# Attention with a 32-bit P: eight tiles with later low-half products, and two of sixteen steps with P as one float

## The chip, the cores and the metric

The kernel runs on one core of one Trainium2 chip. The metric is device time in microseconds. The core's engines are called as in the profile: PE (TensorE, matrix products), PEld (its weight loads), DVE (VectorE), ACT (ScalarE), POOL (GpSimd) and SP (SyncE, which starts transfers).

## The reference

The computation is one transformer-like layer with 2048 rows of 512 features, modulated by a condition vector `c`. Attention has 32 heads of 16 features, all in float32:

```
mod = (silu(c) @ w_mod) split into sa, ca, ga, sb, cb, gb
h   = layernorm(x) * (1 + ca) + sa
q, k, v = split(h @ A_wqkv)                 # 32 heads of 16
p   = softmax(q k^T * 0.25)                 # 2048 x 2048 per head
x   = x + ga * ((p v) @ A_wo)
h   = layernorm(x) * (1 + cb) + sb
x   = x + gb * mixer(h)                     # gelu layers w1, w2 with shifts, then w3, w4
```

## The kernel before

The kernel keeps nearly float32 accuracy while it uses fast matmul forms. Weights and activations are split into a high and a low part in fp32r, and three products replace one fp32 product.

Attention is cut into 64 **units** (`units`, line 946): four chunks of 512 queries times 16 pairs of heads. A unit has 16 **steps**, one per 128 keys, and a step has two **half-steps**, one per head of the pair (j = 0, 1). A half-step does two things on PE, as a *row pair*: the scores of its own step (`score_part`, tile `sc`, line 1012) and, 24 steps ahead (`LEAD`), scores in the other orientation for a coming unit's row maxima (`max_part`, tile `mb`, line 996). The two use different halves of the array's rows. DVE reduces `mb` to maxima (line 992). ACT takes the exponential of `sc` and writes it as a 32-bit integer into a tile of P, `pt` (line 1008); the exponent is shifted so that the integer has up to 26 bits.

P times V then goes in two halves of that integer. The high 16 bits are read in place as fp16 numbers; four matmuls per step (line 1086, one **group**, 32 columns each and hence side by side in the array) multiply them with V, which is held in three bf16 parts (`vst`). The low 16 bits are first made fp16 in place by `p_low` on POOL (line 1061), or on ACT (lines 1058 and 1059, shown in the profile as L156) when POOL's planned clock is more than 200 ns behind ACT's. One group of four matmuls per *pair* of steps multiplies them (line 1083). All products of a unit add up in one PSUM bank, `pv`. After the unit ACT copies it to `ac` (line 1103), PE sorts it (`ot`, line 1113), and ACT, DVE and POOL divide by the row sums (lines 1120 to 1128). The next unit's first group waits for that copy.

There are eight PSUM banks: one for `pv`, seven shared by `sc`, `mb` and `ot`. Tiles of P come from a ring of six (`NPT`).

The order of instructions on every engine is written out by a planner in Python (`Sched`), which keeps a clock per engine from fixed costs (a row pair 232 ns, a group 240, a maximum 605, an exponential 480, a low half 1345 on POOL and 1150 on ACT; a transfer its bytes at 360 per ns, then 2200 ns). Engines run their instructions in that order. The main loop (line 1602) goes by **blocks** of three half-steps (`GRP`): three row pairs, then the groups that are due. What is due stands in the list `pvs` (line 1600): for each pair of steps the high group of the first, that of the second, then the low group. An entry is taken two blocks (`LAG`) after its half-step has passed: half-step 2s for the first high group, 2s + 2 for the second and for the low group. V for a unit is fetched six steps ahead (`load_v`), Q and K 32 steps ahead.

The query chunks' remaining work (output projection, mixer) is the *tail*. Its memory pool `fa` is set up at the end of unit 15, but it is used only near the end of attention and after it, with tiles `xn`, `xf` and `xb` among others.

Of the kernel before, what the change touches and what calls it, by code (L numbers as in the profile page):

```python
# [105 lines left out]
LNG = (1, 3)  # L106
LNC = 2
VP = 2
XB = 4


# [219 lines left out]
def kernel(ctx, tc, A_x, A_wqkv, A_wo, B_w1, B_w2, B_w3, B_w4, c, w_mod, out):  # L331
# [635 lines left out]
            load_rows(kst[u % 3], j, Ks, h, slice(0, S), slice(0, S))  # L967

    def load_v(u):
        vst[u] = at.tile([P, NKT, 192], BF16, name="vst", tag="vst", bufs=2)  # L970
        sch.dma(dma.dma_start, vst[u], Vs[units[u][1]])

    sm = Slots(NSM)
    e_exp, e_hi, e_low, v_free, acs = {}, {}, {}, [0.0], []

    def bank(nm):
# [3 lines left out]
    def max_part(m, j):  # L980
# [14 lines left out]
                max_fin(u)  # L995
        return ready, lambda: te.matmul(b, lhs, kst[u % 3][r, c * CH:(c + 1) * CH], start=True, stop=True), after  # L996

    def score_part(s, j):

        u, kt = divmod(s, NKT)  # L1000
        if j == 0:
            pt[s] = at.tile([P, 2, CH], I32, name="pt", tag="pt", bufs=NPT)
        x, b = bank("sc")
        ready, sm.t[x] = sm.t[x], LATE
        r = slice(64 * j, 64 * j + 64)

        def after(e):
            ea = sch.crit("A", 480, e + PX, lambda: act.activation(pt[s][:, j], b, AF.Exp))  # L1008
            sm.t[x] = ea + XP["A"]
            if j:  # L1010
                e_exp[s] = e_hi[s] = ea
        return ready, lambda: te.matmul(b, kst[u % 3][r, kt * P:(kt + 1) * P], qst[u][r], start=True, stop=True), after  # L1012

    def row_pair(s, j):
# [48 lines left out]

    def pv_ready(s, lo):

        return max(e_low[s], e_low[s + 1]) if lo else max(e_hi.pop(s), v_free[0] if s % NKT == 0 else 0.0)

    def pv_part(s, lo):


        u, kt = divmod(s, NKT)
        if kt == 0 and not lo:
            pv[u] = ap_.tile([P, CH], F32, name="pv", tag="v", bufs=1)
        v, acc = vst[u], pv[u]

        def mms():
            for j in range(2):
                for i in range(2):
                    r = 64 * j + 32 * i
                    if lo:  # L1080
                        c = 128 + 32 * j + (0 if i else 8)
                        n = min(32, 192 - c)
                        te.matmul(acc[r:r + n, :], v[:, kt + i, c:c + n].bitcast(F16), pt[s + i].bitcast(F16)[:, j, 0::2],  # L1083
                                  start=False, stop=kt == NKT - 2, skip_group_check=True)
                    else:
                        te.matmul(acc[r:r + 32, :], v[:, kt, r:r + 32], pt[s].bitcast(F16)[:, j, 1::2],  # L1086
                                  start=kt == 0, stop=False, skip_group_check=True)
# [135 lines left out]
    def pool_of(ci):  # L1223
        return fa if ci < NB or (ci - NB) % 2 else tp
# [58 lines left out]
    def tail(ci):  # L1283
# [91 lines left out]
        def normed(key, t, rs):  # L1375
            tag = xtag(key, t)
            xlive[tag] = xlive.get(tag, 0) + 1
            x = xn[key, t] = (tp if tag == "x4" else fa).tile([P, D], F32, name="xn", tag=tag, bufs=XN[tag])
            y = xbt[t]
            return ln_apply(x, y, rs), mark((key, t))  # L1380

# [15 lines left out]
        for i, t in enumerate(new):  # L1397
            yield lambda: ci != 1 or i < HOLD or ("xn4", 2) in done
            yield lambda: sch.room() and xn_room("xn", t) and t in x1t and sch.now() >= arr.get(("x1", t), 0.0) and (ci < 2 or ("z", t - 2 * TPC) in done)
            yield from wo_mm(i, range(KT))  # L1400
            b = banks.pop(i)
            x1 = x1t[t]
            xb = xbt[t] = pool_of(ci).tile([P, D], F32, name="xb", tag="xb", bufs=XBF if pool_of(ci) is fa else XBT)

            def x1_add(x1=x1, b=b):
                dve.tensor_tensor(x1, x1, b, op=OP.add)
                sch.free(b)

            r, m, ops = ln_ops(x1, True)
            r2, ops2 = ln_ops(xb)  # L1410

            def center(xb=xb, x1=x1, m=m, ops=ops):
                ops[0][2]()
                sch.late = sch.put("G", 464, sch.T["D"] - cD() + XX, ops[1][2]) + XX
                dve.scalar_tensor_tensor(xb, x1, m[:, 0:1], cbrow, op0=OP.subtract, op1=OP.mult)
# [181 lines left out]


    blocks = [list(range(i, min(i + GRP, 2 * NS))) for i in range(-2 * LEAD, 2 * NS, GRP)]
    pvs = [x for s in range(0, NS, 2) for x in ((s, 0), (s + 1, 0), (s, 1))]  # L1600
    due = 0.0
    for k, blk in enumerate(blocks + [[]] * (LAG + CPER)):
        if blk and blk[0] <= LENDS <= blk[-1]:
            sch.most = MOST
        for x in blk:
            if x % 2 == 0:
                if x == blk[0]:
                    before(x // 2)
                if x >= 0 and x % 32 == 0:
                    drain(("shift", x // 32))  # L1610
        if acs:
            ac_copy()
        row = [divmod(x, 2) for x in blk if x < 2 * NS]
        s0 = row[0][0] if row else 0
        col = []
        if k >= LAG and (k % CPER == 0 or not blk):

            x = (blocks[min(k - LAG, len(blocks) - 1)] or [-1])[-1]
            while pvs and 2 * (pvs[0][0] + pvs[0][1]) < x and not (col and pvs[0][0] % NKT == 0 and not pvs[0][1]):
                col.append(pvs.pop(0))  # L1620
        t, start = CIN, 0.0
        need = sum((s >= 0) + (s + LEAD < NS) for s, _ in row)
        sch.flush(need)
        banks = sorted(sm.t)
        n = 0
        for s, i in row:
            n += (s >= 0) + (s + LEAD < NS)

            start = max(start, banks[n - 1 + 2 * (s < 0)] - t)
            t += CROW  # L1630
        t += CMID
        for s, i in col:
            start = max(start, pv_ready(s, i) - t)
            t += CCOL
        sch.gap(start)
        sch.flush(need)
        sch.T["P"] = max(sch.T["P"], start) + CIN
        low = sorted(e_exp)
        for s, i in row:
            for fn in row_pair(s, i):  # L1640
                fn()
        for x in blk[1:]:
            if x % 2 == 0:
                before(x // 2)
        for s in low:
            p_low(s)
        sch.T["P"] += CMID
        for s, i in col:
            pv_part(s, i)
        sch.T["P"] += COUT  # L1650
        for e in "ADG":
            sch.misc(e, max(sch.T["P"], sch.T[e]) + TOLE[e])
        if s0 < 0:
            sch.fill(LEADB / 2 * len(blk))
        elif sch.gens:
            late = s0 >= NS - T0S
            due += RATE3 if late else RATE if s0 < NS // NC else RATE2
            if due >= (BURST3 if late else BURST if s0 < NS // NC else BURST2):
                sch.fill(due)
                due = 0.0  # L1660
        if 2 * (NS // NC) - 1 in blk:
            for key in (("v", 1), ("kq", 3), ("q", 0), ("q", 1), "pieces"):
                drain(key)
            qpx.close()
            sch.gapmin = GAPMIN2
            ot = o0x.enter_context(tc.tile_pool(name="ot", bufs=1, side="right"))
            for ci in range(1, NC):
                oh[ci] = ot
                osb[ci] = ot.tile([P, TPC, D], F32, name=f"osb{ci}", tag=f"osb{ci}", bufs=1)
            fa = o0x.enter_context(tc.tile_pool(name="fa", bufs=1, side="right"))  # L1670
            big = {"A4": fa.tile([P, 4 * KT * 2 * P], F32R, name="A")}
            big["A"] = big["A4"]
        if blk and blk[0] <= 2 * (NS - T0L) <= blk[-1]:
            sch.add(tail_loads())
        if blk and blk[0] <= 2 * (NS - T0S) <= blk[-1]:
            sch.add(tail(0))
# [54 lines left out]
```

## Time and profile before

| | |
|---|---|
| median of 3 runs | 2019.44 us (2016.7 to 2020.83) |
| profiled execution | span 2019.7 us; the profile gives no other time of it |
| instructions | 41655 |
| PE busy | 1934.4 us, 96% |
| DVE busy | 1656.3 us, 82% |
| ACT busy | 1510.2 us, 75% |
| POOL busy | 1571.9 us, 78% |
| PE's granted clock | 0.992 of full speed |

The shares are over the whole span. The first part (to about 500 us) mixes projections with attention, the middle is attention alone, and after about 1500 us comes the tail, in which PE works almost alone. A change to attention is to be read in the middle. In the lists of groups a row gives line, engine, operation, tiles (written <- read), shapes and count, then busy time in us and the mean duration in ns, then the idle time before it and who ended it. A matmul's duration includes its way through the array; how far apart matmuls start says what they cost.

### The profile page before, as it was taken

To read this page: it belongs to the slowest core of one execution; us is meant where nothing else is said; L and a number is where in the kernel's file an instruction comes from. 1 tells how busy PE (TensorE), PEld (TensorE's weight loads), DVE (VectorE), ACT (ScalarE), POOL (GpSimd) and SP (SyncE) were. 2 spreads that over 40 slices of the span, in tenths; PEclk is the share of its full clock that TensorE was granted. 3 is DMA by queue.
4 is the path that set the end of the run, shared out by engine and by line. 5 is a ranking of instruction groups with operands and counts; after the bars stand their busy time and mean duration, and the time that the engine had idled before them with its cause. 6 is when DMAs were issued, how large, how long until landed. Compare 5 with 4: busy or idle time off the path is not lost.

```text
span 2019.7 us, 41655 instructions
## 1 busy us (share of the span) xinstructions
PE 1934.4 (96%) x14456; PEld 1162.1 (58%) x14456; DVE 1656.3 (82%) x2979; ACT 1510.2 (75%) x3085; POOL 1571.9 (78%) x1488
## 2 busy tenths in 40 slices
PE   7999999999999999999999999999998999999999
PEld 5755545454444444444444444444455878898998
DVE  6398888879999999999999999999975886556443
ACT  6438987768999999999999999999985544344443
POOL 6349988879999999999999999999996554435222
PEclk9989999999999999999999999999999999999999
DMA  8777675445343434444443435354414676553541
GB/s 295 233 204 192 151 187 155 135 130 124 86 92 87 91 88 83 96 82 97 81 98 75 104 72 107 72 136 126 99 46 158 230 261 265 226 200 116 201 153 68
DMA packets 185508, 278.01 MB, mean 138 GB/s; under 512 B 117104, under 2 KB 127856, under 8 KB 169008
## 3 DMA queue, kind: packets, MB, share of 16 engines
q1 hardware_dynamic: 181792, 267.20, 49.1%
q10 hardware_dynamic: 2304, 4.20, 0.6%
q0 software_dynamic: 1200, 3.93, 0.5%
q8 instruction: 115, 1.88, 0.4%
q14 instruction: 97, 0.79, 0.1%
HBM read 211.81 MB, written 62.91 MB: 136 GB/s over the span
## 4 chain that ended last, share of the span: by engine, by line
PE 61%; DVE 16%; ACT 9%; issue 6%; POOL 4%; DMA 3%; SPq 0%; ACTq 0%; POOLq 0%; DVEq 0%
PE mb L996 13%; DVE mx L992 12%; PE pv L1086 9%; PE sc L1012 8%; ACT pt L1008 7%; PE w L363 5%; PE w L359 5%; PE w L361 5%; PE pv L1083 4%; PE ot L1113 3%; POOL pt L1061 2%; PE xT L1247 1%; POOL trs L1356 1%; PE v L359 1%; DMA wr<-Ws 1%
## 5 line engine op out<-in xcount | busy, mean ns | idle before, releaser
L1061 POOL TENSOR_SCALAR pt<-pt 128x1024 f16<-128x1024 uint16 x953 | 1248.3, 1367 | 79.9 <-ACT pt L1008 76.7
L992 DVE TENSOR_REDUCE mx<-mb 128x1 f32<-128x512 f32 x2048 | 1250.0, 681 | 72.7 <-PE mb L996 63.5
L1008 ACT ACTIVATE pt<-sc 128x512 int32<-128x512 f32 x2048 | 1060.9, 614 | 123.5 <-PE mb L996 97.1
L996 PE MATMUL mb<-kst,qtl 62*128 62x512 f32 x2048 | 781.1, 461 | 20.5 <-ACT pt L1008 10.0
L1012 PE MATMUL sc<-qtl,kst 64*128 64x512 f32 x2048 | 739.3, 449 | 4.6 <-DVE mx L992 1.8
L996 PEld LDWEIGHTS mb<-kst,qtl 62*128 62x128 f32 x2048 | 358.9, 193 | 233.7 <-ACT pt L1008 160.4
L1012 PEld LDWEIGHTS sc<-qtl,kst 64*128 64x128 f32 x2048 | 336.6, 185 | 185.4 <-DVE mx L992 118.7
L1086 PE MATMUL pv<-pt,vst 128*32 128x512 f16 x4096 | 384.8, 397 | 20.6 <-ACT ac L1103 20.6
L1460 POOL TENSOR_TENSOR g<-sq,g 128x256 fp32r<-128x256 f32 (+1 forms) x124 | 96.8, 785 | 188.9 <-ACT g L1459 176.6
L1083 PE MATMUL pv<-pt,vst 128*32 128x512 f16 (+1 forms) x2048 | 220.8, 389 | 2.5 <-POOL pt L1061 2.4
L1086 PEld LDWEIGHTS <-vst 128*32 128x32 bf16 x4096 | 91.8, 93 | 227.2 <-issue 208.8
L361 PE MATMUL w<-A,wr 128*128 128x256 f32 (+1 forms) x520 | 153.4, 295 | 0.3 <-DVE A L349 0.3
L359 PE MATMUL w<-A,wr 128*128 128x256 f32 (+1 forms) x520 | 153.2, 295 | 0.3 <-ACT A L353 0.3
L363 PE MATMUL w<-A,wr 128*128 128x256 f32 (+1 forms) x520 | 153.1, 294 | 0.0
L1456 ACT ACTIVATE sq<-w 128x256 f32<-128x256 f32 (+1 forms) x130 | 52.1, 401 | 127.0 <-PE w L363 117.5
L363 PE MATMUL w<-wr,g 128*128 128x512 f32 x270 | 106.5, 394 | 3.1 <-POOL g L1460 3.1
L359 PE MATMUL w<-wr,g 128*128 128x512 f32 x270 | 106.9, 396 | 1.8 <-DMA wr<-Ws 1.8
L361 PE MATMUL w<-wr,g 128*128 128x512 f32 x270 | 106.1, 393 | 0.0
L1438 DVE SCALAR_TENSOR_TENSOR sq<-sq,w 128x256 f32<-128x256 f32 (+1 forms) x130 | 58.1, 449 | 56.5 <-ACT sq L1458 56.3
L359 PEld LDWEIGHTS w<-A,wr 128*128 128x128 f32 x520 | 98.7, 190 | 1.7 <-ACT A L353 0.5
L361 PEld LDWEIGHTS w<-A,wr 128*128 128x128 f32 x520 | 98.7, 190 | 1.6 <-DVE A L349 0.5
L363 PEld LDWEIGHTS w<-A,wr 128*128 128x128 f32 x520 | 98.6, 190 | 0.5 <-issue 0.5
(156 smaller groups left out, 2131.6 us busy)
## 6 DMA issues: line engine op xcount, KB each, us to landing
wr<-Ws SPq DMA_DIRECT2D x66, 1024.0 KB, 5.2
vst<-Vs SPq DMA_DIRECT2D x64, 768.0 KB, 5.7
kst<-Ks SPq DMA_DIRECT2D x126, 384.0 KB, 6.1
Ws<-wr SPq DMA_DIRECT2D x14, 1024.0 KB, 5.0
qtl<-Qs SPq DMA_DIRECT2D x128, 96.0 KB, 4.3
Vs<-vt SPq DMA_DIRECT2D x32, 384.0 KB, 4.2
Ks<-qk SPq DMA_DIRECT2D x16, 512.0 KB, 3.8
Qs<-qk SPq DMA_DIRECT2D x16, 512.0 KB, 3.0
```

Source lines behind the costliest of these rows:

```text
L359: te.matmul(o, lh, rh, start=first, stop=False)
L361: te.matmul(o, lh, rl, start=False, stop=False)
L363: te.matmul(o, ll, rh, start=False, stop=last)
L992: end = sch.crit("D", 605, e + PX, lambda: dve.reduce_max(mxs[u][:, j, g, c:c + 1], b, axis=AX.X))
L996: return ready, lambda: te.matmul(b, lhs, kst[u % 3][r, c * CH:(c + 1) * CH], start=True, stop=True), after
L1008: ea = sch.crit("A", 480, e + PX, lambda: act.activation(pt[s][:, j], b, AF.Exp))
L1012: return ready, lambda: te.matmul(b, kst[u % 3][r, kt * P:(kt + 1) * P], qst[u][r], start=True, stop=True), after
L1061: e_low[s] = XP["G"] + sch.crit("G", 1345, ready, lambda: pool.tensor_scalar(o, i, 0.5, 1.0, op0=OP.mult, op1=OP.mult))
L1083: te.matmul(acc[r:r + n, :], v[:, kt + i, c:c + n].bitcast(F16), pt[s + i].bitcast(F16)[:, j, 0::2], start=False, stop=kt == NKT - 2, skip ...
L1086: te.matmul(acc[r:r + 32, :], v[:, kt, r:r + 32], pt[s].bitcast(F16)[:, j, 1::2], start=kt == 0, stop=False, skip_group_check=True)
L1113: te.matmul(b[:, t * n:(t + 1) * n], ac[:, t * P:(t + 1) * P], smat.rearrange("p j d -> p (j d)"), start=True, stop=True)
L1460: ("G", cG(n), lambda: pool.tensor_tensor(lo, sq, hi, op=OP.subtract)), (None, 0, end), bank=b)
```

## The change

First, the ring of P tiles has eight members from step 264 to 983: six as before and two laid into the tail's tiles `xn` and `xf`, which are empty then. In the same steps the low group of a pair of steps is due up to three half-steps later (not for the last pair of a unit).

Second, in units 17 to 60 the steps 4 and 5 of the 16 are handled otherwise (`full`). ACT writes the exponential of such a step as one float per element into `pfull` (in the tail's `xb`); there is no low half, and it takes no tile of the ring. V of these two key tiles is made once per unit on POOL: `vfull` is the three bf16 parts of V as float32, times 2^-40, queued by `load_v` when the transfer of V is planned to have landed. Instead of the high groups and the low group of the two steps (three groups of four matmuls) there are four parts (`pv_full`), two per step. Each part covers 256 of the 512 queries and consists of two fp32 products, 64 output rows per head. Their gates are half-steps 1, 4, 7 and 10 after the first of the two steps, so they fall into different blocks as a rule; the planner charges 460 ns each.

The tail's `xn`, `xf` and `xb` become fixed slices of three tiles, with as many slots as before, so that the loans above are possible. The diff without that last part:

```
+WIDE = range(S // CH * 64 + 8, 984)
+LOWLAG = 3
+FU = range(17, 61)
+FK = 4
+FGATE = (1, 4, 7, 10)
+CFULL = 460.0
...
     def load_v(u):
-        vst[u] = at.tile([P, NKT, 192], BF16, name="vst", tag="vst", bufs=2)
-        sch.dma(dma.dma_start, vst[u], Vs[units[u][1]])
+        v = vst[u] = at.tile([P, NKT, 192], BF16, name="vst", tag="vst", bufs=2)
+        e = sch.dma(dma.dma_start, v, Vs[units[u][1]])
+        if u in FU:
+            sch.chain(("G", 360, lambda: pool.tensor_scalar(vfull[u % 2], v[:, FK:FK + 2, 0:128], 2.0 ** -20, 2.0 ** -20,
+                                                            op0=OP.mult, op1=OP.mult)), prio=0, ready=e)
+
+    def full(s):
+        return s // NKT in FU and s % NKT in (FK, FK + 1)
...
+    def new_pt(s):
+        if s in WIDE:
+            i = pn[0] % (NPT + len(ptx)) - NPT
+            pn[0] += 1
+            if i >= 0:
+                pt[s] = ptx[i]
+                return
+        pt[s] = at.tile([P, 2, CH], I32, name="pt", tag="pt", bufs=NPT)
...
-        if j == 0:
-            pt[s] = at.tile([P, 2, CH], I32, name="pt", tag="pt", bufs=NPT)
+        if full(s):
+            p = pfull[s % 2][j]
+        else:
+            if j == 0:
+                new_pt(s)
+            p = pt[s][:, j]
...
-            ea = sch.crit("A", 480, e + PX, lambda: act.activation(pt[s][:, j], b, AF.Exp))
+            ea = sch.crit("A", 480, e + PX, lambda: act.activation(p, b, AF.Exp))
             sm.t[x] = ea + XP["A"]
             if j:
-                e_exp[s] = e_hi[s] = ea
+                e_hi[s] = ea
+                if not full(s):
+                    e_exp[s] = ea
...
+    def pv_full(s, n):
+
+        u, kt = divmod(s, NKT)
+        c = slice(256 * n, 256 * n + 256)
+
+        def mms():
+            for j in range(2):
+                r = slice(64 * j, 64 * j + 64)
+                te.matmul(pv[u][r, c], vfull[u % 2][:, kt - FK, r], pfull[s % 2][j][:, c], start=False, stop=False,
+                          skip_group_check=True)
+        sch.put("P", CFULL, 0.0, mms)
...
-    pvs = [x for s in range(0, NS, 2) for x in ((s, 0), (s + 1, 0), (s, 1))]
+    pvs = []
+    for s in range(0, NS, 2):
+        if full(s):
+            pvs += [(2 * s + x, s + i // 2, 2 + i % 2) for i, x in enumerate(FGATE)]
+            continue
+        low = 2 * s + 2 + (min(LOWLAG, 2 * (NKT - 2 - s % NKT)) if s in WIDE else 0)
+        pvs += [(2 * s, s, 0), (2 * s + 2, s + 1, 0), (low, s, 1)]
+    pvs.sort(key=lambda x: x[0])
...
+            pfull += [[xbs[:, 2 * i + j] for j in range(2)] for i in range(2)]
+            vfull += [xns["xn"][:, 2, 256 * i:256 * i + 256].rearrange("p (k d) -> p k d", k=2) for i in range(2)]
+            ptx += [x[:, 0:2].bitcast(I32) for x in xns.values()]
```

More of the change, by code (lines that the diff above doesn't have):

```diff
@@ L969, in load_v @@
     def load_v(u):
-        vst[u] = at.tile([P, NKT, 192], BF16, name="vst", tag="vst", bufs=2)
-        sch.dma(dma.dma_start, vst[u], Vs[units[u][1]])
+        v = vst[u] = at.tile([P, NKT, 192], BF16, name="vst", tag="vst", bufs=2)
[5 more added lines that the diff above has]
+        return s // NKT in FU and s % NKT in (FK, FK + 1)
     sm = Slots(NSM)
+    ptx = []
+    vfull, pfull = [], []
     e_exp, e_hi, e_low, v_free, acs = {}, {}, {}, [0.0], []
@@ L996, in max_part @@
         return ready, lambda: te.matmul(b, lhs, kst[u % 3][r, c * CH:(c + 1) * CH], start=True, stop=True), after
+    pn = [0]
+    def new_pt(s):
[6 more added lines that the diff above has]
+        pt[s] = at.tile([P, 2, CH], I32, name="pt", tag="pt", bufs=NPT)
     def score_part(s, j):
         u, kt = divmod(s, NKT)
-        if j == 0:
-            pt[s] = at.tile([P, 2, CH], I32, name="pt", tag="pt", bufs=NPT)
+        if full(s):
[4 more added lines that the diff above has]
+            p = pt[s][:, j]
         x, b = bank("sc")
@@ L1064, in pv_ready @@
     def pv_ready(s, lo):
+        if lo > 1:
+            return e_hi[s]
         return max(e_low[s], e_low[s + 1]) if lo else max(e_hi.pop(s), v_free[0] if s % NKT == 0 else 0.0)
+    def pv_full(s, n):
[7 more added lines that the diff above has]
+        sch.put("P", CFULL, 0.0, mms)
     def pv_part(s, lo):
@@ L1377, in normed @@
             xlive[tag] = xlive.get(tag, 0) + 1
-            x = xn[key, t] = (tp if tag == "x4" else fa).tile([P, D], F32, name="xn", tag=tag, bufs=XN[tag])
+            if tag == "x4":
+                x = tp.tile([P, D], F32, name="xn", tag=tag, bufs=XN[tag])
+            else:
+                x = xns[tag][:, xnum[tag] % XN[tag]]
+                xnum[tag] += 1
+            xn[key, t] = x
             y = xbt[t]
@@ L1402, in tail @@
             x1 = x1t[t]
-            xb = xbt[t] = pool_of(ci).tile([P, D], F32, name="xb", tag="xb", bufs=XBF if pool_of(ci) is fa else XBT)
+            xb = xbt[t] = xbs[:, t % XBF] if pool_of(ci) is fa else tp.tile([P, D], F32, name="xb", tag="xb", bufs=XBT)
             def x1_add(x1=x1, b=b):
@@ L1618 @@
             x = (blocks[min(k - LAG, len(blocks) - 1)] or [-1])[-1]
-            while pvs and 2 * (pvs[0][0] + pvs[0][1]) < x and not (col and pvs[0][0] % NKT == 0 and not pvs[0][1]):
-                col.append(pvs.pop(0))
+            while pvs and pvs[0][0] < x and not (col and pvs[0][1] % NKT == 0 and not pvs[0][2]):
+                col.append(pvs.pop(0)[1:])
         t, start = CIN, 0.0
@@ L1633 @@
             start = max(start, pv_ready(s, i) - t)
-            t += CCOL
+            t += CFULL if i > 1 else CCOL
         sch.gap(start)
@@ L1648 @@
         for s, i in col:
-            pv_part(s, i)
+            if i > 1:
+                pv_full(s, i - 2)
+            else:
+                pv_part(s, i)
         sch.T["P"] += COUT
@@ L1671 @@
             big = {"A4": fa.tile([P, 4 * KT * 2 * P], F32R, name="A")}
+            xbs = fa.tile([P, XBF, D], F32, name="xbs")
+            xns = {k: fa.tile([P, XN[k], D], F32, name=k) for k in ("xn", "xf")}
+            xnum = {"xn": 0, "xf": 0}
+            pfull += [[xbs[:, 2 * i + j] for j in range(2)] for i in range(2)]
+            vfull += [xns["xn"][:, 2, 256 * i:256 * i + 256].rearrange("p (k d) -> p k d", k=2) for i in range(2)]
+            ptx += [x[:, 0:2].bitcast(I32) for x in xns.values()]
             big["A"] = big["A4"]
```

## The prediction

> **What bounds the kernel now.** I read the busy time by stretches first. In the middle of attention nothing is idle; where it ends, everything but PE thins out.
>
> ```profile
> 600.00:700.00 100.00, 96.50 (x824) 45.54 (x824) 96.14 (x168) 92.87 (x185) 95.66 (x83) 1.00 0.43 91
> ...
> 1500.00:1600.00 100.00, 88.37 (x548) 66.69 (x545) 67.17 (x133) 55.20 (x113) 64.95 (x83) 0.97 0.45 159
> ```
>
> PE, PE's loads, DVE, ACT and POOL stand in that order. Four engines at 93 to 97% do not say which one sets the pace, so the second view is the groups of instructions from 600 to 1400 us, pure attention.
>
> ```profile
> L992 DVE TENSOR_REDUCE mx<-mb 128x1 f32<-128x512 f32 x1257 | 764.1, 681 | 26.7 <-PE mb L996 21.0 <-PE sc L1012 2.9
> L1128 DVE RECIPROCAL rc<-sm 128x8 f32<-128x8 f32 x39 | 7.6, 195 | 5.7 <-ACT sm L1120 5.7
> L1042 DVE TENSOR_REDUCE mf<-mx 128x8 f32<-128x32 f32 x39 | 7.0, 180 | 0.1
> ...
> L1061 POOL TENSOR_SCALAR pt<-pt 128x1024 f16<-128x1024 uint16 x577 | 751.1, 1363 | 27.2 <-ACT pt L1008 25.0
> L1124 POOL TENSOR_TENSOR osb<-sm,rc 128x128 f32<-128x128 f32 x39 | 15.9, 409 | 2.8 <-DVE rc L1128 2.8
> L1045 POOL TENSOR_TENSOR nm<-mf,nm 128x8 fp32r<-128x8 f32 x39 | 7.9, 203 | 2.3 <-ACT nm L1044 2.0
> ...
> L1008 ACT ACTIVATE pt<-sc 128x512 int32<-128x512 f32 x1257 | 648.4, 615 | 47.4 <-PE mb L996 39.0 <-PE sc L1012 2.0 <-POOL pt L1061 0.8
> L156 ACT ACTIVATE pt<-pt 128x1024 f16<-128x1024 uint16 x53 | 72.9, 1375 | 0.0
> L1103 ACT ACTIVATE ac<-pv 128x512 f32<-128x512 f32 x39 | 24.3, 624 | 0.0
> ```
>
> A unit (one head pair against one query chunk, 16 steps) has 32 maxima, so the window holds 1257 / 32 = 39.28 units of 800 / 39.28 = 20.37 us, and a block (three half-steps, 1.5 steps) takes 1.91 us. The chain of waits has a piece in which DVE alone sets the pace:
>
> ```profile
> 1224.05 17.87 DVE mx L992 x30
> ```
>
> That is 17.87 / 30 = 0.596 us per maximum, 1.79 us per block. DVE therefore needs 32 x 0.596 + 0.195 + 0.180 = 19.45 us per unit and loses 0.92. POOL works (751.1 + 15.9 + 7.9) / 39.28 = 19.73 us per unit: 577 / 39.28 = 14.7 low halves and two small operations; the other 53 / 39.28 = 1.35 low halves go to ACT. DVE is the floor, POOL and ACT sit right under it. The waits of that window show how the 0.92 us arise:
>
> ```profile
> PEld mb L996 <- ACT pt L1008: 115.8, 340, 0.8
> PEld sc L1012 <- DVE mx L992: 84.8, 219, 0.5
> ...
> PE pv L1086 <- ACT ac L1103: 15.2, 13, 1.2
> ```
>
> PE's loads wait for PSUM banks that ACT or DVE has not emptied, and every third unit PE stops for the copy of the accumulator. One such stop in order of time, ACT, then DVE, then PE:
>
> ```profile
> 849.51 1.35 ACT L156 ACTIVATE pt<-pt 128x1024 f16<-128x1024 uint16 x1
> 850.71 0.60 ACT L1103 ACTIVATE ac<-pv 128x512 f32<-128x512 f32 x1
> ```
>
> ```profile
> 845.33 6.66 DVE L992 TENSOR_REDUCE mx<-mb 128x1 f32<-128x512 f32 x11
> 852.71 1.89 DVE L992 TENSOR_REDUCE mx<-mb 128x1 f32<-128x512 f32 x3 [0.72 <-PE mb L996]
> ```
>
> ```profile
> 847.47 0.49 PE L1012 MATMUL sc<-qtl,kst 64*128 64x512 f32 x1
> ...
> 848.38 0.41 PE L1086 MATMUL pv<-pt,vst 128*32 128x512 f16 x4
> 848.62 0.40 PE L1083 MATMUL pv<-pt,vst 128*32 128x512 f16 x4
> 848.94 0.50 PE L996 MATMUL mb<-kst,qtl 62*128 62x512 f32 x1
> ...
> 849.69 0.51 PE L996 MATMUL mb<-kst,qtl 62*128 62x512 f32 x1
> ...
> 851.35 0.64 PE L1086 MATMUL pv<-pt,vst 128*32 128x512 f16 x8 [1.16 <-ACT ac L1103]
> ...
> 852.14 0.50 PE L1012 MATMUL sc<-qtl,kst 64*128 64x512 f32 x1
> ...
> 853.25 0.41 PE L1086 MATMUL pv<-pt,vst 128*32 128x512 f16 x4
> 853.60 1.08 PE L1113 MATMUL ot<-smat,ac 128*128 128x34 f32 x8
> 854.61 0.51 PE L996 MATMUL mb<-kst,qtl 62*128 62x512 f32 x1
> ...
> 855.50 0.41 PE L1086 MATMUL pv<-pt,vst 128*32 128x512 f16 x4
> 855.74 0.40 PE L1083 MATMUL pv<-pt,vst 128*32 128x512 f16 x4
> 855.97 0.41 PE L1086 MATMUL pv<-pt,vst 128*32 128x512 f16 x4
> 856.30 0.50 PE L1012 MATMUL sc<-qtl,kst 64*128 64x512 f32 x1
> ```
>
> A low half on ACT holds up the accumulator's copy; PE idles 1.16 us, and DVE runs dry for 0.72 us. The same rows give PE's own need: an unstalled block with two groups of P V products takes 848.94 - 847.47 = 1.47 us, with three 856.30 - 854.61 = 1.69 us. So a block is about 1.01 us plus 0.23 per group. DVE's 1.79 us leave PE 0.1 to 0.3 us per block. That margin decides this case.
>
> **The change, part by part.** The page gives no time of the profiled execution but its span, 2019.7 us; the median of the three runs is 2019.44, so I work from 2019.7. The runs spread over 0.2%, about what a measurement of this kernel can tell from no change. Units 17 to 60 are changed: 44 units.
>
> *Relief of POOL and ACT.* Two of 16 low halves per unit disappear: 2 x 1.30 = 2.6 us (751.1 / 577). One operation that scales V comes in, 128 x 256. No row shows it; the nearest are a smaller one, L1124 above (128 x 128, 0.41 us), and one of its size with two inputs:
>
> ```profile
> L787 POOL TENSOR_TENSOR vt<-vr,vt 128x256 bf16<-128x256 f32 x32 | 22.6, 710 | 36.6 <-ACT vt L786 36.4
> ```
>
> I take 0.55 us, between the two. With all 14 low halves on POOL its work is 14 x 1.30 + 0.40 + 0.20 + 0.55 = 19.35 us, just under DVE's floor. The planner charges POOL 16 x 1345 + 600 = 22.1 us per unit now and, at 20.4 us, must hand (22.1 - 20.4) / 1.345 = 1.3 low halves to ACT, which the trace confirms (1.35). With the change it charges 14 x 1345 + 600 + 360 = 19.8 us. Fourteen steps in a row still build up a backlog, so I expect not zero but some 0.7 on ACT. Worth: at most DVE's whole 0.92 us per unit, at least nothing (if another wait is late next). I take the stop at the accumulator, 15.2 / 39.28 = 0.39 us per unit. Once it goes, the bank waits on DVE's maxima are late next.
>
> *P as one float.* The exponentials keep shape and source; L1103 writes float from the same shape in 0.624 us against 0.615, so nothing. PE loses three groups per unit (four high and two low halves' products are one group per high step and one per low pair): 3 x 0.23 = 0.69 us. It gains four parts, each of two fp32 products of 256 columns. What one costs is seen where the prologue multiplies in fp32:
>
> ```profile
> 40.28 1.46 PE L806 MATMUL vb<-wab,gcol 128*128 128x256 f32 x6
> ...
> L806 PE MATMUL vb<-wab,gcol x16: 377/379/483, 40.3 to 127.7; 128*128 128x256 f32 x16
> ```
>
> Line 806 is called eight times and shows 16 matmuls, so an fp32 product is two; six take 1.46 us of which the last lasts 0.38, so 0.216 us apart. A part is then four matmuls: a1 and a2 for one head, b1 and b2 for the other, in different column halves. The order is a1, a2, b1, b2. Groups of four in different columns start together (the x4 rows), but every later group waits 0.23 us for the earlier one and none overtakes. So a2 waits for a1, b1 can only start with a2, and b2 after b1: three slots, 0.65 us. Bounds: two slots, 0.43, if the heads overlap wholly; four, 0.86, if fp32 in two column halves does not overlap at all. I take 0.65. The planner charges 0.46. The Trainium skill, "TensorE: Matmul & The Clock Gate", Part 3, says that matmuls start and end strictly in program order; the rows agree.
>
> A part also has another shape than its neighbours. From the group at 853.25 to the full-width products at 853.60 pass 0.35 us instead of 0.23: 0.12 for a change of shape, which I add once per part: 0.77 us. The Trainium skill, "TensorEngine Tiling (Array Packing)", Key Properties, says that changing the tiling mode drains the array; by it the 0.12 is paid on both sides of each part, 4 x 0.12 = 0.5 us more per unit.
>
> Placed by the gates, the four parts lie in four blocks next to 6.3 groups (mean of the three alignments of a unit). These need 4 x (1.01 + 0.77) + 6.3 x 0.23 = 8.57 us of PE against 4 x 1.79 = 7.16 of DVE: 1.41 us too long. DVE's queue covers some of it. After PE's last row pair at 849.69 DVE ran on until 851.99 (845.33 + 6.66), 2.30 us; a new result needs 852.71 - 852.14 = 0.57 us from its pair's start, so the stretch from the last pair to the next may last 1.73 us. With two groups it is 0.9 us, so up to 0.8 us is in reserve, where PE was ahead. I count two thirds, 0.56; bounds 0 and 0.8. Loss 1.41 - 0.56 = 0.85 us per unit.
>
> *Later low products and eight tiles.* The first page has PE's low products and, in its last part, V's transfer:
>
> ```profile
> L1083 PE MATMUL pv<-pt,vst 128*32 128x512 f16 (+1 forms) x2048 | 220.8, 389 | 2.5 <-POOL pt L1061 2.4
> ...
> vst<-Vs SPq DMA_DIRECT2D x64, 768.0 KB, 5.7
> ```
>
> No DMA moves and no queue is passed; low products come a block later on PE. PE hardly waits for POOL (2.4 us in the whole span) and ACT hardly for a tile (0.8 us above), so there is nothing to win. The two edits are cover for a new wait: on POOL the scaling of V waits for V's transfer, 5.7 us to land where the planner reckons 2.2 us of transfer and 2.2 us of latency, 4.4. The low halves queue behind it, up to 1.3 us per unit, and the low products behind those; their new delay of three half-steps, 1.9 us, hides that. Without this cover it would be at most 1.3 us.
>
> *Sum.* -0.39 + 0.85 = +0.46 us per unit, times 44: 20 us. 2019.7 + 20 = **2040 us**, slower.
>
> **Rivals.** *Heads overlap wholly* (faster). A part costs 0.43 + 0.12 = 0.55; the four blocks need 4 x 1.56 + 1.45 = 7.69, 0.53 too long, all of it inside the reserve of 0.56. The relief stays: 0.39 to 0.92 us per unit, 17 to 40 us, 1980 to 2003; I take 0.45, 2000. For it: groups of four do run together. Against it: each fp32 product is two matmuls in sequence. It decides as soon as a part takes under about 0.55 us. The Trainium skill, "TensorE: Matmul & The Clock Gate", Part 3, counts matmuls in different column tiles as one plus 4 ns each; by that rule a part would take two slots.
>
> *No overlap.* 0.86 + 0.12 per part adds 4 x 0.21 = 0.84: +1.3 us per unit, 57 us, 2077.
>
> *The low halves stay on ACT.* If the planner still hands 1.35 per unit to ACT, the relief is 0: 0.85 x 44 = 37 us, 2057.
>
> *The two sides cancel.* A fuller reserve (0.8) and a relief of 0.6 give 1.41 - 0.8 - 0.6 = 0, 2020.
>
> **How the numbers follow.** Forecast 0.42 (2024 to 2060), whole overlap 0.32, low halves on ACT 0.07, no overlap 0.09, cancelling 0.10. Faster is the whole overlap, with 0.02 of the cancelling case; slower the forecast and its two companions; the rest within 0.2%. The range leaves out a tenth at each end: the best of the whole overlap and the dearest of no overlap, 1988 to 2064. The likeliest case's own range is 2024 to 2060.
>
> **What would show it.** Right: matmuls of the new form starting at 0, 0.216, 0.22 and 0.43 us; DVE's idle time gathered in the four blocks of steps 4 and 5; ACT's low halves well below 1.35 per unit; POOL's share down. Wrong: four matmuls of a part within 0.43 us, blocks that stay near 1.79 us, or units of 17 to 60 shorter than 20.37 us.

## The result, and the profile after

The changed kernel takes 2212.11 us (median of four runs, 2208.94 to 2214.8), 1.096 times the kernel before (95% interval 1.094 to 1.097). The forecast had the direction; 148 us of the time lie above the top of its range. The profiled execution spans 2208.6 us, and TensorE's mean granted clock in it is 0.948, against 0.992 before.

The groups of the whole page give the first lead (busy time and mean duration, then idle time before the group and what ended it):

```profile
L1006 DVE TENSOR_REDUCE mx<-mb 128x1 f32<-128x512 f32 x2048 | 1259.6, 680 | 252.7 <-PE mb L1010 224.5
...
L1043 PE MATMUL sc<-qtl,kst 64*128 64x512 f32 x2048 | 733.1, 456 | 143.9 <-DMA qtl<-nm 139.8
```

Nothing in the prediction speaks of the second row. PE's scores wait 139.8 us for the transfer `qtl<-nm`, by which `shift_rows` writes the negated row maxima into two rows of each head's queries. The stretches of 100 us, to be held against those quoted of before (PE, its loads, DVE, ACT, POOL, clock):

```profile
700.00:800.00 100.00, 88.07 (x721) 40.25 (x720) 83.14 (x143) 77.59 (x155) 77.52 (x69) 0.95 0.36 77
800.00:900.00 100.00, 83.48 (x647) 38.24 (x649) 74.18 (x128) 70.75 (x140) 65.57 (x59) 0.86 0.33 67
```

and of before, for the second of them:

```profile
800.00:900.00 100.00, 97.72 (x828) 46.10 (x824) 96.75 (x170) 93.13 (x185) 96.12 (x82) 1.00 0.44 91
```

All four engines thin out together in the middle of attention, and the clock falls with them: the whole machine stops now and then. The waits from 600 to 1400 us (total, times, longest) say how often:

```profile
DVE mx L1006 <- PE mb L1010: 128.9, 88, 9.6
...
PE sc L1043 <- DMA qtl<-nm: 103.3, 11, 9.8
```

Eleven waits of up to 9.8 us in 800 us, one in every third unit (18, 21, ... 60: 15 in all). The stop at the accumulator's copy, `PE pv <- ACT ac`, 15.2 us before, is not among the waits of that window. One stop in order of time, first POOL, SP and PE, each line with its start and length:

```profile
937.75 0.20 POOL L1076 TENSOR_TENSOR nm<-mf,nm 128x8 fp32r<-128x8 f32 x1 [0.55 <-ACT nm L1075]
```

```profile
945.24 0.30 SPq L141 DMA_DIRECT2D qtl<-Qs  x1
945.59 1.07 SPq L141 DMA_DIRECT2D kst<-Ks  x1
946.75 0.38 SPq L141 DMA_DIRECT2D qtl<-Qs  x1
947.19 0.42 SPq L141 DMA_DIRECT2D kst<-Ks  x1
947.70 8.04 SPq L141 DMA_DIRECT2D qtl<-nm  x8
```

```profile
945.22 0.51 PE L1010 MATMUL mb<-kst,qtl 62*128 62x512 f32 x1
945.23 0.50 PE L1043 MATMUL sc<-qtl,kst 64*128 64x512 f32 x1
945.66 0.64 PE L1131 MATMUL pv<-pt,vst 128*32 128x512 f16 x8
956.05 0.76 PE L1043 MATMUL sc<-qtl,kst 64*128 64x512 f32 x1 [9.75 <-DMA qtl<-nm]
```

The rows are computed at 937.95. They are not sent then. SP's queue holds the loads of Q and K for a later unit in front of them, and these wait for a buffer that the running unit still reads: they start as PE works on its last row pair (945.24). The eight small transfers of the rows follow at 947.70, and the next unit's first score cannot start before they have landed. A unit without a stop has the same five entries of SP in the other order:

```profile
917.58 4.98 SPq L141 DMA_DIRECT2D qtl<-nm  x8
924.07 0.31 SPq L141 DMA_DIRECT2D qtl<-Qs  x1
924.42 0.42 SPq L141 DMA_DIRECT2D kst<-Ks  x1
```

The kernel before has this order in every unit; one of them:

```profile
940.47 4.98 SPq L135 DMA_DIRECT2D qtl<-nm  x8
945.87 0.31 SPq L135 DMA_DIRECT2D qtl<-Qs  x1
946.23 0.42 SPq L135 DMA_DIRECT2D kst<-Ks  x1
```

In the code, `shift_rows` is the end of a chain that the planner releases in passing, when it fills an idle stretch of PE's plan, or at the latest when the main loop drains `("shift", u)` at the unit's first half-step. Where that half-step opens a block, which is so in every third unit (32 half-steps, blocks of three), the loop calls `before` first, and `before` queues the loads. What changed is that the planner, with fp32 parts charged at 460 ns and low groups moved, no longer found an idle stretch in time (read from the planner's code; the first kernel below shows only that an earlier release cures it).

The rest of the profile after, in the groups from 600 to 1400 us. The window holds 1038 / 32 = 32.4 units, so the 23 + 6 + 3 low halves on ACT are 0.99 per unit:

```profile
L1109 PE MATMUL pv<-xbs,xn 128*64 128x256 f32 x524 | 85.5, 405 | 0.0
...
L1037 ACT ACTIVATE xbs<-sc 128x512 f32<-128x512 f32 x128 | 70.1, 698 | 1.8 <-PE mb L1010 1.5 <-PE sc L1043 0.4
...
L162 ACT ACTIVATE pt<-pt 128x1024 f16<-128x1024 uint16 x23 | 31.6, 1372 | 0.0
...
L979 POOL TENSOR_SCALAR xn<-vst 128x256 f32<-128x256 bf16 x33 | 13.4, 406 | 2.6
...
L162 ACT ACTIVATE xf<-xf 128x1024 f16<-128x1024 uint16 x6 | 8.2, 1374 | 0.0
...
L162 ACT ACTIVATE xn<-xn 128x1024 f16<-128x1024 uint16 x3 | 4.1, 1378 | 0.0
```

A part costs PE as follows (timeline of PE):

```profile
900.57 0.41 PE L1128 MATMUL pv<-pt,vst 128*32 128x512 f16 x4
900.91 0.65 PE L1109 MATMUL pv<-xbs,xn 128*64 128x256 f32 x4
901.50 0.41 PE L1131 MATMUL pv<-pt,vst 128*32 128x512 f16 x4
```

The group before is followed after 0.34 us instead of the usual 0.24, and the next instruction comes 0.58 us after the part's first. Within the part the four matmuls start at 0, 0.007, 0.267 and 0.273 us (medians).

### The profile page after: what moved, and what is told of

It is laid out like the page before. It is cut to its first block, busy times and chain, and to the rows that moved or that the text cites. A ratio compares the mean times of both kernels' runs of the same rounds, so it can differ in the third digit from the quotient of the medians.

```text
span 2208.6 us, 41772 instructions
## 1 busy us (share of the span) xinstructions
PE 2012.0 (91%) x14632; PEld 1186.4 (54%) x14632; DVE 1668.0 (76%) x2979; ACT 1501.1 (68%) x3071; POOL 1504.7 (68%) x1458
## 4 chain that ended last, share of the span: by engine, by line
PE 70%; DVE 9%; DMA 7%; ACT 5%; POOL 5%; issue 3%; SPq 1%; ACTq 0%; POOLq 0%; DVEq 0%
PE mb L1010 15%; PE sc L1043 12%; PE pv L1131 10%; DVE mx L1006 6%; PE pv L1128 5%; PE w L365 5%; PE w L369 5%; PE w L367 5%; DMA qtl<-nm 5%; PE pv L1109 5%; PE ot L1158 3%; ACT pt L1037 2%; POOL pt L1092 2%; SPq L141 1%; DMA wr<-Ws 1%
## 5 line engine op out<-in xcount | busy, mean ns | idle before, releaser
L1092 POOL TENSOR_SCALAR pt<-pt 128x1024 f16<-128x1024 uint16 x732 | 969.7, 1365 | 228.6 <-ACT pt L1037 224.6
L1037 ACT ACTIVATE pt<-sc 128x512 int32<-128x512 f32 x1556 | 826.1, 614 | 241.0 <-PE mb L1010 202.6
L1043 PE MATMUL sc<-qtl,kst 64*128 64x512 f32 x2048 | 733.1, 456 | 143.9 <-DMA qtl<-nm 139.8
L1010 PE MATMUL mb<-kst,qtl 62*128 62x512 f32 x2048 | 769.9, 465 | 10.1 <-ACT pt L1037 3.1
L1131 PE MATMUL pv<-pt,vst 128*32 128x512 f16 x3112 | 301.6, 404 | 5.6 <-ACT ac L1148 5.6
L1128 PE MATMUL pv<-pt,vst 128*32 128x512 f16 (+1 forms) x1556 | 165.0, 407 | 1.0 <-POOL pt L1092 1.0
L1092 POOL TENSOR_SCALAR xn<-xn 128x1024 f16<-128x1024 uint16 x76 | 103.1, 1357 | 53.4 <-ACT xn L1037 53.1
L1037 ACT ACTIVATE xn<-sc 128x512 int32<-128x512 f32 x158 | 90.4, 620 | 49.3 <-PE mb L1010 45.0
L1109 PE MATMUL pv<-xbs,xn 128*64 128x256 f32 x704 | 114.8, 405 | 0.0
L1092 POOL TENSOR_SCALAR xf<-xf 128x1024 f16<-128x1024 uint16 x71 | 96.4, 1357 | 9.2 <-ACT xf L1037 8.3
```

Of the source, the lines that this page charges most:

```text
L1037: ea = sch.crit("A", 480, e + PX, lambda: act.activation(p, b, AF.Exp))
L1092: e_low[s] = XP["G"] + sch.crit("G", 1345, ready, lambda: pool.tensor_scalar(o, i, 0.5, 1.0, op0=OP.mult, op1=OP.mult))
L1109: te.matmul(pv[u][r, c], vfull[u % 2][:, kt - FK, r], pfull[s % 2][j][:, c], start=False, stop=False, skip_group_check=True)
```

## The experiments

All times are medians; ratios are to the kernel before, with 95% intervals. "Unit" is the mean distance between every 32nd maximum over units 20 to 55: 20.38 us before. My theory after the result (A) was that the order of SP's queue, with its 15 stops, is the whole loss. Rival B: the fp32 parts cost PE what was forecast, and the stops only hide it. Rival C: the scaling of V on POOL waits for V's transfer and holds up the row maxima, so that the order on SP does not matter. The runs led to three separate things: the order of SP's queue costs 15 stops, the floats lose by PE's time, and the ring with later low products gains.

**Floats and ring apart.** Three kernels: the changed one with the planner's marks released after every block (so the rows go out early); the ring and later low products alone; the floats alone.

```
# after_marks, at the end of the loop over blocks
+        sch.marks()
# ring_only
-FU = range(17, 61)
+FU = range(0)
# float_only
-WIDE = range(S // CH * 64 + 8, 984)
+WIDE = range(0)
```

> The changed kernel, with the planner's due marks fired after every block, so that the small transfer of the negated maxima is queued on SP ahead of the next unit's Q and K again. Theory A (15 stops of PE, one in every third unit, because that transfer stands behind loads that wait for the running unit's last scores; each costs its wait of some 9.9 us and about 3 us at the halved clock behind it): PE waits for the transfer 0 times, the granted clock is back at 0.99, and the time is 2212 - 15 x 12.9 = 2018 us, within 10. Rival B (the fp32 parts cost PE what was forecast, and the stops only hide it): 2040 us. Rival C (the scaling of V on POOL, waiting for V's transfer, holds up the negated maxima): the order on SP does not matter and the time stays within 20 us of 2212.

> Eight tiles of P and the later low products alone; no step has P as floats. Its order on SP is that of the kernel before. Theory A: no long stop, 2018 us within 6, since PE waited for low halves only 2.4 us before. A theory that the eight tiles or the later low products themselves cost the 194 us: near 2210 us.

> P as one float in steps 4 and 5 of units 17 to 60, with six tiles of P and low products as early as before. Its order on SP is that of the kernel before. Theory A: no long stop; between 2010 and 2045 us, from what the float steps give and take alone. Rival B: 2040 us or above. Rival C, the scaling of V: 2150 us or more, since the scaling is in this kernel as well.

Measured: 2046.04 us (1.011, 1.009 to 1.014) with the marks, unit 20.87; 2003.15 us (0.990, 0.988 to 0.993) for the ring alone, unit 19.91; 2073.91 us (1.026, 1.023 to 1.028) for the floats alone, unit 21.29. None of the three has the wait for `qtl<-nm` among its waits from 600 to 1400 us, and in their traces no unit's rows stand behind the next four loads. So each half of the change keeps the rows in front and only both together lose it; and the ring alone is a little faster than the kernel before. Theory A's times were missed in all three (2018 us, 2018 us, and at most 2045 us for the floats): the stops are not the whole loss, and the floats cost time of their own. Rival C falls, since the floats alone scale V as well and do not stop.

Both half kernels stop once elsewhere. PE waits 3.9 us for K (`kst<-Ks`) near 1400 us with the floats alone, after the DMA engines were busy throughout (share 1.00, 329 GB/s from 1385 to 1395 us), and 3.2 us with the ring alone. The units around it are some 9 us longer in all with the floats, and some 5 us with the ring, than others of their kind. The kernel before, the changed kernel and the one with the rows drained first (below) have no such wait; why it arises was not examined. The waits of the floats alone, then of the ring alone, from 600 to 1400 us:

```profile
DVE mx L1006 <- PE mb L1010: 36.9, 70, 1.2
...
PE pv L1131 <- ACT ac L1148: 19.9, 24, 1.2
```

```profile
DVE mx L1006 <- PE mb L1010: 14.1, 34, 3.0
DVE mx L1006 <- PE sc L1043: 3.1, 10, 0.6
DVE rc L1173 <- ACT sm L1165: 0.6, 1, 0.6
```

The stop at the accumulator's copy is still there with floats alone, although ACT has only 0.99 low halves per unit, and it is gone with the ring alone, although ACT has 1.66. The number of low halves on ACT does not decide it.

**The stop without the change.** The kernel before, with the rows queued behind the loads in units 18, 21, ... 60:

```
+LATEU = range(18, 61, 3)
...
-                  (None, 0, shift_rows), mark(("shift", u)), prio=0, ready=sch.T["D"])
+                  *([mark(("nm", u))] if u in LATEU else [(None, 0, shift_rows), mark(("shift", u))]), prio=0, ready=sch.T["D"])
...
+                    if x // 32 in lateu:
+                        drain(("nm", x // 32))
+                        lateu.pop(x // 32)()
+                        done.add(("shift", x // 32))
```

> The kernel before, with one thing of the change alone: in units 18, 21, ... 60 the transfer of the negated maxima is queued behind the next loads of Q and K. Theory A: 15 stops of about 10 us and the halved clock behind each, 2018 + 15 x 13 = 2213 us, within 15. Rivals B and C: within 10 us of 2018, since neither float steps nor the scaling of V are in it.

Measured: 2196.95 us, 1.086 (1.084 to 1.088), clock 0.952: 176 us more than the kernel before, 11.7 per stop (the expectation had 13), with nothing of the change in it, neither floats nor the scaling of V. Its waits from 600 to 1400 us:

```profile
DVE mx L993 <- PE mb L997: 131.3, 69, 9.6
...
PE sc L1013 <- DMA qtl<-nm: 96.1, 11, 9.2
```

**The change without the stop.** The changed kernel; the rows are drained before the loads are queued:

```
                 if x == blk[0]:
+                    if x >= 0 and x % 32 == 0:
+                        drain(("shift", x // 32))
                     before(x // 2)
```

> The changed kernel with another cure for the order on SP: at a unit's start the planner waits for the negated maxima before it queues the next unit's loads; nothing else is fired earlier. If the stops are the order on SP and nothing else, it is as fast as the kernel with marks after every block, 2046 us within 8, with no wait of PE for that transfer above 1 us. If firing marks after every block has a price of its own (in that kernel POOL waited 17 us in 800 for V's transfer before it scaled V), it is faster: some 2025 to 2035 us.

Measured: 2039.8 us, 1.009 (1.007 to 1.011), clock 0.994, unit 20.80. SP at the start of one of the units that stopped, and the waits from 600 to 1400 us:

```profile
941.83 5.01 SPq L141 DMA_DIRECT2D qtl<-nm  x8
949.37 0.31 SPq L141 DMA_DIRECT2D qtl<-Qs  x1
949.72 0.42 SPq L141 DMA_DIRECT2D kst<-Ks  x1
```

```profile
DVE mx L1006 <- PE mb L1010: 27.5, 66, 1.0
...
DVE mx L1006 <- PE sc L1043: 8.5, 10, 0.9
...
PE pv L1131 <- ACT ac L1148: 3.1, 13, 0.5
...
PE sc L1043 <- DMA qtl<-nm: 0.2, 1, 0.2
```

Taking the stops out saves 2212.1 - 2039.8 = 172 us, 11.5 per stop; putting them in where nothing else changed cost 11.7. This settles what the order on SP costs.

**What the ring's gain needs.** Eight tiles without the later low products, and the later low products with six tiles (both from the ring alone, without floats):

```
# tiles_only
-LOWLAG = 3
+LOWLAG = 0
# low_only, in new_pt
-        if s in WIDE:
+        if False:
```

> Eight tiles of P alone: low products as early as before, no float steps. Eight tiles and later low products together took 2003 us. If the tiles are what helps (exponentials that no longer wait for a tile): 2003. If the later low products are: within 5 us of 2020, since ACT waited for a tile only 0.8 us in 800 before.

> Later low products alone, with six tiles, no float steps. If the later products help by themselves: 2003 us. If they need the tiles: a tile is held three half-steps longer, so exponentials wait for tiles and the time is above the kernel before, 2030 us or more, with waits of ACT for PE's low products that the kernel before does not have.

Measured: 2020.77 us, 1.000 (0.999 to 1.002) for the tiles alone, where the stop at the copy stays; 2134.55 us, 1.056 (1.055 to 1.058) for the low products alone, unit 22.98. One wait of each, in that order:

```profile
PE pv L1131 <- ACT ac L1148: 16.4, 14, 1.2
```

```profile
ACT pt L1037 <- PE pv L1128: 125.2, 197, 1.0
```

With six tiles, ACT waits for a low product to give its tile back, 125.2 us in 800; the two further tiles remove that wait. Neither edit gains by itself, both together gain 0.47 us per unit.

**Is a part's time on PE what the floats cost?** Each part issued twice (on the kernel with the marks):

```
-            for j in range(2):
+            for j in (0, 1, 0, 1):
```

> The changed kernel with marks after every block (2046 us), and each fp32 part issued twice, so that steps 4 and 5 count double in the result: four more matmuls per part, in pairs 0.26 us apart, 0.52 us. If PE is what is late in the float steps' blocks: up to 4 x 0.52 x 44 = 92 us more, 2115 to 2140. If PE has slack there and the float steps cost something else (POOL, ACT, the planner's order): under 2070.

Measured: 2111.05 us, 1.045 (1.043 to 1.046), unit 22.51. The doubled part's matmuls start in pairs at 0, 0.267, 0.483 and 0.698 us, and the next instruction follows at 1.014 us instead of 0.583: 0.431 us more, 1.72 per unit, 76 us in 44 units, not the 92 that I had reckoned. Of these, 65 us show in the time and 1.65 per unit in the units' length. So a further addition to PE goes through nearly whole. It says nothing of what covers the single parts: a reserve that these had used up would let the second ones through as well. With the rows drained first, PE is busy 796.1 of the 800 us from 600 to 1400 and DVE 757.7; before, it was 774.9 and 767.5. By these figures PE, not DVE, is now the engine that hardly stops.

**Fewer changes of shape, or a lump?** One part of 512 columns per float step in place of two of 256, at the first and third gate (on the kernel with the rows drained first):

```
-CFULL = 460.0
+CFULL = 920.0
...
-        c = slice(256 * n, 256 * n + 256)
+        c = slice(0, CH)
...
-            pvs += [(2 * s + x, s + i // 2, 2 + i % 2) for i, x in enumerate(FGATE)]
+            pvs += [(2 * s + x, s + i, 2) for i, x in enumerate((1, 7))]
```

> The rows sent ahead of the next loads, and each fp32 step's four parts of 256 columns as two of 512 at the first and third place, so that half as many changes between the two kinds of product are left: two steps lose four of eight changes (.10 each by the starts) and their parts' last slots, about .3 to .5 us of TensorE a unit. If the floats' loss is TensorE's time (binding some 75 in 100 of it, by the doubled parts), 10 to 17 us come off 2040: 2023 to 2030. Rival: what counts is the lump that one block of twelve score halves has to carry against VectorE's queue; a lump of 1.1 us in place of .6 then costs at least what the changes save, and the time is 2040 or more.

Measured: 2035.38 us, 1.006 (1.004 to 1.008), unit 20.70. Between the two theories: a wide part takes 1.009 us against 2 x 0.583, which with two changes of shape fewer is some 0.4 us of PE per unit, and 0.10 of it arrived. Two waits of it from 600 to 1400 us, against the 27.5 and 8.5 above:

```profile
DVE mx L1006 <- PE mb L1010: 34.2, 57, 1.3
...
DVE mx L1006 <- PE sc L1043: 6.2, 8, 1.2
```

The waits are fewer but longer (1.3 in place of 1.0 us). By the distances between maxima (what exceeds 0.597 us from one to the next), those beside the parts lose 0.25 us more per unit than with four parts, and the others 0.36 us less: beside the parts the lump costs more than the changes of shape save, and the gain is elsewhere. ACT also has 0.34 low halves per unit in place of 0.99, so the planner moved other things too. This run does not separate the two theories.

**How much reserve pays.** Ring alone with ten tiles and six places (and the rows drained first); ring alone with two places:

```
# ten_tiles
-LOWLAG = 3
+LOWLAG = 6
...
-            ptx += [x[:, 0:2].bitcast(I32) for x in xns.values()]
+            ptx += [x[:, 0:2].bitcast(I32) for x in xns.values()] + [xbs[:, 2 * i:2 * i + 2].bitcast(I32) for i in range(2)]
# lag_two
-LOWLAG = 3
+LOWLAG = 2
```

> Ring alone (no floats) with ten tiles in place of eight and the low products six places later in place of three, the rows sent ahead of the next loads. VectorE still idles 17.2 us in 800 us (.43 us a unit) with eight tiles, 14.1 of it before the first mask tile behind a wait for TensorE. If more reserve goes on paying, up to .43 x 44 = 19 us come off 2003: 1984 to 1995. If the stop at the accumulator's copy was all that the reserve could take, which is my theory, 2003 within 5.

> Ring alone with the low products two places later in place of three. The stop at the accumulator's copy was there with no place (16.4 us in 800) and gone with three. If each place takes its share of it, a third of the 17 us is lost again: about 2009. If two are enough for the last low half of a unit, 2003 within 3.

Measured: 2042.6 us, 1.010 (1.007 to 1.012), unit 20.71, for ten tiles; 2017.27 us, 0.998 (0.997 to 0.999), unit 20.25, for two places. Both expectations missed. The waits of ten tiles, then of two places, from 600 to 1400 us:

```profile
DVE mx L1006 <- PE mb L1010: 37.1, 68, 2.5
...
PE pv L1131 <- ACT ac L1148: 11.3, 19, 1.2
ACT sm L1165 <- PE ot L1158: 10.6, 26, 0.6
```

```profile
DVE mx L1006 <- PE mb L1010: 18.0, 41, 2.0
DVE rc L1173 <- ACT sm L1165: 9.3, 13, 0.7
```

With two places the stop at the copy is gone as well, but DVE now waits 9.3 us for ACT's row sums (0.6 with three places): another wait took its place. With ten tiles the stop at the copy is back. So the ring's gain is no matter of reserve alone. That it hangs on where the low products fall beside the end of a unit is my reading, and not shown. Which of the two edits of the ten-tile kernel brought the stop back, or whether draining the rows first takes part, was not separated.

## Why the prediction was wrong, point by point

**The step that failed** is in "Later low products and eight tiles": "No DMA moves and no queue is passed ... so there is nothing to win." Both halves of it fell. A DMA did move: the rows of the maxima went behind four loads on SP in every third unit, though the diff touches neither. That is 172 of the 193 us by which the kernel became slower, shown from both sides (11.5 us per stop taken out, 11.7 put in). The sentence was argued from the diff. What a planner emits is decided by its clocks, though, and every cost that the change alters can move any later instruction; the step needed the question which transfers the planner releases only when it finds time, and what can get in front of them in the queue. And there was something to win: the two edits together gain 0.47 us per unit, 16 to 18 us.

**The relief** came near in size only by luck (forecast 0.39 us per unit; the ring and the low products gain 0.47) and was wrong in cause. I put it down to ACT's fewer low halves in the float steps. The floats alone brought these down to 0.99 per unit (forecast 0.7) and left the stop at the copy at 19.9 us. The ring and the later low products took it away, with more low halves on ACT than before. Whether the fewer low halves bring a relief elsewhere was not measured apart.

**The float part.** "The order is a1, a2, b1, b2 ... three slots, 0.65 us" was wrong: two matmuls of different heads start 0.007 us apart, so a part has two slots, 0.27 and 0.31 us. That is the mechanism of the first rival, and the rule of the Trainium skill named there ("TensorE: Matmul & The Clock Gate", Part 3) agrees with these starts. The change of shape, 0.12 in the forecast, measures 0.10 behind a group and nothing behind a row pair (0.33 us, as without a part). More of it may lie inside: within the doubled parts the inner pairs follow at 0.216 us, so two plain slots would be 0.43 us, and the other 0.15 of the 0.58 lie at a part's first (0.05) and last slot (0.10). By the starts some 58 of 100 parts follow a group: 0.58 + 0.06 = 0.64 us per part in place of 0.77. PE's addition is then 4 x 0.64 - 3 x 0.23 = 1.87 us per unit, not 2.39.

**The reserve.** 0.56 us were to be covered by DVE's queue. With the measured part the forecast's own form gives 4 x (1.01 + 0.64) + 1.45 - 7.16 = 0.89 us too long, and the floats cost as much: 0.89 per unit on top of the ring (20.80 against 19.91), 0.91 alone (21.29 against 20.38). For the floats alone this fits a reserve of nothing. But 1.45 stands for 6.3 further groups in the four blocks, which the trace of the floats alone has (6.3 per unit); with the later low products only 4.7 stand there (counted with the rows drained first). With these the form gives 4 x 1.65 + 4.7 x 0.23 - 7.16 = 0.52, within the reserve of 0.56, and the loss should have been nothing. It was 0.89, so the form itself does not carry it. The 0.8 us were read at one stop of PE, and at a full queue: there DVE ended 2.30 us after the start of PE's last row pair, while over units 20 to 55 of the kernel before the median is 2.01, and one block in ten has 2.31 or more. By the median the reserve is 2.01 - 0.57 - 0.9 = 0.54 us. Why a queue of that length does not shorten the loss stays open.

**The sum.** Without the stops the kernel takes 2039.8 us, against 2040. This agreement is luck: the part was taken too dear, the further groups too many, a reserve was counted that did not show, and the relief came from another edit. The full account, 2019, less 17 (ring and low products), plus 37 (floats), plus 172 (stops), is 2211; it must add up, since each term is the difference between two of the kernels measured. In another order the terms differ: the floats alone cost 53 us, 0.91 x 44 = 40 of them in the units and some 9 at the stop for K.

**Of the rivals**, whole overlap had the right mechanism at the wrong price: a part takes 0.64 with its change of shape, and its cost shows where that rival had it covered. The heads did overlap, so "no overlap" falls, and the two sides did not cancel. Low halves did leave ACT (0.99 against 1.35), yet the floats alone show no relief at the copy, which is what the rival "the low halves stay on ACT" had as its outcome. No rival had a transfer out of order.

**What would show it.** DVE's idle time did gather where the parts run: without the stops, about 0.8 us more per unit than before lies between the maxima beside them (counting what exceeds 0.597 us from one maximum to the next). ACT's low halves fell and POOL's share too (691.6 us of 800 with the rows drained first, 767.8 before). The matmuls' starts showed the slot order wrong, as the text said they would.

**The smaller terms.** V's scaling takes 0.41 us (taken: 0.55) and waits for nothing worth naming (2.6 us in the groups above). In the kernel with the marks, which emits it sooner, it waits 17.4 us for V's transfer from 600 to 1400 us, at most 3.8 us at a time: the wait that the forecast described exists, and does not decide. The exponential that writes float was put at the old duration. It takes 0.70 us against 0.61 to 0.62 for the others in the same window, 0.3 us of ACT per unit; its share of the loss was not measured by itself, but with the floats alone it takes 0.64 us and these cost 0.91 per unit all the same.

## What to carry to other kernels

Where a planner writes the order out, compare the order of the DMA queues before and after a change, even if the diff names no transfer, and look first at small transfers whose reader is near and which stand beside loads that wait for a buffer. A queue in front of the engine that sets the pace is a reserve only if it is full when it is needed: read it over many blocks, and count in the new trace what stands in the blocks that you summed. Doubling the added work shows what a further addition costs, not what covered the first. And when a change has two halves, try each alone: here one was worth 16 us as it stood (2003 us), and the other cost 37 on top of it.

## What was not expected of the hardware

Each stop costs more than its wait: 139.8 us of waits cost 172. The clock through one stop, in stretches (engines as above, then the granted clock, the DMA share and GB/s):

```profile
945.70:956.00 10.30, 0.59 (x10) 0.08 (x8) 1.54 (x3) 0.94 (x2) 2.67 (x3) 0.72 0.59 96
956.00:959.00 3.00, 2.90 (x14) 1.14 (x14) 1.77 (x3) 1.51 (x3) 0.16 (x1) 0.50 0.03 0
...
961.00:966.00 5.00, 5.00 (x40) 2.63 (x40) 2.98 (x5) 3.29 (x7) 3.72 (x3) 0.71 0.38 127
```

The clock falls to half during the wait and stays there for some 8 us of work after it; the periods at half clock last 10.2 or 13.7 us, and this one, of 13.7, begins about 4 us after PE's last products. After a stop with a period of 10.2 us, some 5 us of work run at half clock. The Trainium skill ("TensorE: Matmul & The Clock Gate", Part 1) has the fall after an idle window of about 3.4 us, which fits, and the return after about 3.4 us of sustained work; here it took some 8 us, or 5.

In fp32, products of two heads in two column halves run together in pairs, 0.007 us apart, while a head's own two passes follow each other at 0.21 to 0.27 us for 256 columns (the first distance of a part is the longer one).
